# Rearranging the opening of a gated linear attention and SoLU kernel: tables, warm-up, block order, masks and the first load of v

## The chip, the cores and the metric

The kernel runs on one core of a Trainium2 chip. The time is the device time of one execution in microseconds (us). Several executions were timed, and their median is the number to predict. One further execution was recorded by the hardware profiler; its span runs from the first to the last instruction of the core. The engines are named PE (TensorE, matmuls), PEld (its weight loads), DVE (VectorE), ACT (ScalarE), POOL (GpSimd) and SP (SyncE, which issues most DMAs).

## The reference

Two blocks follow each other. The first is a linear attention with a decay for every channel, over 4 batches, 8 heads, 768 tokens and a head dimension of 48. The second is an MLP on the 3072 tokens with 384 inputs and 1024 hidden units.

```python
for t in range(S):
    state = alpha[:, :, t, :, None] * state + np.einsum('bhd,bhe->bhde', k[:, :, t], v[:, :, t])
    y[:, :, t] = np.einsum('bhd,bhde->bhe', q[:, :, t], state)
...
x = np.ascontiguousarray(attn_out.transpose(0, 2, 1, 3)).reshape(B * S, H * D)
h = x @ w_in
e = np.exp(h - h_max)
sm = e / (np.sum(e, axis=-1, keepdims=True) + 1e-09)
solu = h * sm
mu = np.mean(solu, axis=-1, keepdims=True)
var = np.mean((solu - mu) ** 2, axis=-1, keepdims=True)
ln = (solu - mu) / np.sqrt(var + 1e-06) * g_ln
return (ln @ w_out).astype(np.float32)
```

## The kernel before

The 768 tokens are cut into six groups of 128 (`g` is 0 to 5); a group holds all four batches. Inside a group the recurrence is solved in blocks. Alpha is scanned backwards and forwards over the 128 tokens (DVE, line 219). Keys and queries are multiplied by these products. PE forms scores from them (line 278), and a triangular mask is multiplied in (line 289). Then PE reads the values out (line 312), and the state is carried on (line 361). A group's 512 columns then go through the MLP: `up_mm` (line 386), exponential, product and square (lines 400 to 402), and `down` (line 497).

The order of all instructions is written out by hand: each engine runs its own instructions in program order, and semaphores connect the engines. The change lies in the opening, which handles group 0 without anything else to overlap it with.

- SP issues the loads at its start: alpha, k and q in two requests each, of 16 runs of 48 numbers for each of 128 partitions (line 153); then v of the first group in one request of 32 such runs (`load_v_first`, line 188); then six requests for the first half of w_in (`fetch`, line 559), in the form of raw 64-bit numbers. POOL spreads v from its landing place `room` into the tile `vn` by two copies (line 190).
- PE starts with 18 matmuls of ones by ones (`warm(18)`, line 667), of which nothing is read. Each float32 matmul is two MATMUL rows in the trace, each with a LDWEIGHTS.
- `turned` (line 165) transposes a source by matmuls with the identity, 12 blocks of four small matmuls: blocks 0 to 7 are the first 32 channels of the 8 heads, and blocks 8 to 11 the last 16 channels of two heads at once, which ACT first gathers into a tile (`ends_of`, line 158). Three tiles of four blocks each leave: `t[0]`, `t[1]` and `t[2]`. That is done for alpha (`an`), the keys (`kn`) and the queries (`qn`).
- For the queries, DVE takes the three tiles in the order 2, 0, 1 (loop at line 685), with a scan ahead of the last. ACT makes two copies of the ends (`apart`, line 242).
- `scores(0, 0)` and `scores(0, 1)` write four batches of four heads each, into four banks per half. DVE multiplies the mask into all eight tiles (`masked`, lines 698 and 699), and goes on with `bits(0)`, which turns raw 64-bit weights of piece 0 into float32.
- `read_values(0)` reads batch after batch: 16 matmuls each, which need both halves of that batch's `sT`; ACT copies each result to `x` (line 348). Then come `gains` (one small transposition, and `g_col` on DVE), `keys_back` (12 transpositions, three copies by ACT, line 299), `in_range(0)` and `in_range(1)` on ACT (lines 576 and 577), and the loop over eight pieces of the MLP, whose first ACT instruction is the exponential at line 400.

Of the kernel before, what the change touches and what calls it, by code (L numbers as in the profile page):

```python
# [9 lines left out]
FP = mybir.dt.float32  # L10
# [4 lines left out]
ALU = mybir.AluOpType  # L15
AX = mybir.AxisListType
P = 128
# [15 lines left out]
def fast_path(ctx, tc, q, k, v, alpha, moe_w_in, moe_w_out, moe_g_ln, out):  # L33
# [12 lines left out]
    nc = tc.nc  # L46
    B, H, S, D = q.shape
# [4 lines left out]
    NP = H // 2  # L52
    NB = H + NP
# [8 lines left out]
    def pool(name, bufs, **kw):  # L62
        return ctx.enter_context(tc.tile_pool(name=name, bufs=bufs, **kw))
# [5 lines left out]
    small = pool("small", 4)  # L69
# [4 lines left out]
    ps_a = pool("ps_a", 1, space=PS)  # L74
# [4 lines left out]
    mask = const.tile([P, P], FP, name="mask")  # L79
# [7 lines left out]
    mhalf = const.tile([P, 1], FP, name="mhalf")  # L87
# [13 lines left out]
    qn = const.tile([P, H, TQ, D], FP, name="qn")  # L101
# [30 lines left out]
    sT = const.tile([P, B, H, P], FP, name="sT")  # L132
# [13 lines left out]
    def by_token(x):  # L146

        return x.rearrange("p h u d -> p (h u d)").rearrange("p (b h d) -> p b h d", b=B, h=H)
# [9 lines left out]
    def ends_of(src, tag=None):  # L158

        ends = ring.tile([P, T4], FP, name=tag) if tag else two.tile([P, T4], FP, tag="two", name="ends")  # L160
        ends = ends.rearrange("p (b d) -> p b d", b=B)
        nc.scalar.copy(out=ends.rearrange("p b (h d) -> p b h d", h=H), in_=by_token(src)[:, :, :, E0:D])
        return ends

    def turned(src, ends, out, blocks=range(NB)):

        x = by_token(src)
        for j in blocks:
            for b in range(B):
                cols = x[:, b, j, 0:E0] if j < H else ends[:, b, E0 * (j - H) : E0 * (j - H) + E0]  # L170
                nc.tensor.matmul(
                    out[j // NP][32 * b : 32 * b + 32, j % NP], lhsT=cols, rhs=ident, start=True, stop=True,
                    tile_position=(0, 32 * b), skip_group_check=True,
                )
# [9 lines left out]
    def load_v_first(slot):  # L184
        x = slots[slot].rearrange("p (n d) -> p n d", d=D)
        y = vn.rearrange("p b h d -> p (b h) d")
        xi, yi = (z.rearrange("p (n i) d -> p i n d", i=2) for z in (x, y))
        nc.sync.dma_start(out=x, in_=v[:, :, 0:P].rearrange("b h p d -> p (b h) d"))
        for i in range(2):
            nc.gpsimd.tensor_copy(out=yi[:, i, :, all_of[i]], in_=xi[:, i])  # L190

# [92 lines left out]
    masks = {}  # L284

    def masked(half, batches=range(B)):
        a = masks[half]
        for b in batches:
            nc.vector.tensor_tensor(  # L289
                out=sT[:, b, half * NP : half * NP + NP], in0=a[b], in1=mask[:, None, :].to_broadcast([P, NP, P]),  # L290
                op=ALU.mult,
            )
# [25 lines left out]
    def read_begin():  # L318
        reading["y"] = {}
        reading["begun"] = set()  # L320
# [118 lines left out]
    def warm(n, ps=ps_o, tag="o"):  # L439
        t = ps.tile([P, 512], FP, tag=tag, name="warm")  # L440
        for i in range(n):
            nc.tensor.matmul(t[:, 0:P], lhsT=ones, rhs=ones, start=True, stop=True)  # L442
# [209 lines left out]
    nc.gpsimd.memset(seed, 0.0)  # L652
    nc.gpsimd.memset(state, 0.0)
    load_v_first(0)
    fetch(0, 3, 2)
    fetch(2, 1, 2)
# [6 lines left out]
    def three(name, where):  # L663
        return [pool.tile([P, NP, P], FP, tag=tag, name=f"{name}{i}") for i, (pool, tag) in enumerate(where)]


    warm(18)
    t = three("tp_a", [(ps_a, "a0"), (ps_a, "a1"), (ps_a, "a2")])
    turned(an, ends_of(an), t)
    for i in range(3):  # L670
# [2 lines left out]
    t = three("tp_k", [(ps_a, "a3"), (ps_h, "h"), (ps_h, "h")])  # L673
# [5 lines left out]
        nc.vector.tensor_tensor(out=kT[:, part], in0=t[i], in1=hk[:, part], op=ALU.mult)  # L679
    scan_on(0, 0)  # L680
    t = three("tp_q", [(ps_o, "o"), (ps_o, "o"), (ps_a, "a0")])
    turned(qn, ends_of(qn), t)

    warm(2, ps_a, "a1")
    for i in (2, 0, 1):
        if i == 1:
            scan_on(0, i)
# [2 lines left out]
            out=qe if i == 2 else qv[:, part], in0=t[i], in1=aT[:, part, 1:SW], op=ALU.mult  # L690
# [4 lines left out]
    t = [x.tile([P, NP, P], FP, tag=n, name="a_" + n) for x, n in ((ps_h, "h"), (ps_o, "o")) for _ in range(2)]  # L695
    scores(0, 1, t)
    read_begin()
    masked(0)
    masked(1)
    bits(0)  # L700
    read_values(0)
# [6 lines left out]
    for f in range(FC):  # L708
        p = 2 + f // 2
# [215 lines left out]
    def compare(out, x, bound, op):  # L925
# [6 lines left out]
        out=chunks[:, :, 2], in0=sums[:, :, 2], scalar=0.25, in1=sums[:, :, 3], op0=ALU.mult, op1=ALU.is_le  # L932
# [6 lines left out]
    else:  # L939
# [9 lines left out]
        out=bad, in0=all_ok[0:1, 0:1], scalar1=float(P * ends[-1]), scalar2=None, op0=ALU.is_lt  # L949
# [415 lines left out]
def kernel(tc, *args):  # L1365

    with ExitStack() as ctx:
        taken = fast_path(ctx, tc, *args)
    with tc.If(taken > 0):
        general_path(tc, *args)  # L1370
# [30 lines left out]
```

## Time and profile before

| what | value |
|---|---|
| median of 4 executions | 385.36 us (383.77, 383.97, 386.75, 387.59) |
| profiled execution, own time | 386.66 us |
| its span | 384.9 us |
| mean granted TensorE clock | 0.991 of full |
| busy: PE, DVE, ACT, POOL | 370.1, 245.4, 144.3, 125.0 us |
| end of the values' matmuls of group 0 (line 312) | 31.9 us after the start |

The profiled execution is 1.3 us slower than the median, and outside of its span lie 1.76 us. The granted clock is the share of full speed that TensorE's clock was given; it is 1.00 or 0.50 in this trace. A waiting time put down to "issue" is one that no semaphore in the trace explains. A line of the chain gives start, length, engine, tile, line and number of instructions; a line of windows gives for each engine the busy time and, in brackets, the number of instructions, then the granted clock, the DMA share and GB/s.

### The profile page before, as it was taken

What the parts mean: (1) busy time and instruction counts of PE and PEld (TensorE: products, weight loads), DVE (VectorE), ACT (ScalarE), POOL (GpSimd) and SP (SyncE); (2) the same over time, 40 slices, a digit from 0 to 9 for tenths busy, and PEclk for the clock granted to TensorE, in tenths of its full rate; (3) what the DMA queues carried; (4) which work ended last, traced back from release to release, by engine and by line L of the source; (5) the groups of instructions that cost most, each with busy time, mean ns of one, the idle gap of its engine ahead of it and who ended that gap; (6) DMA issues with size and microseconds to landing.
All of it is one profiled execution on the core that took longest, in us unless ns stands there. A gap on an engine that the chain in (4) does not pass through costs nothing.

```text
span 384.9 us, 10525 instructions
## 1 busy us (share of the span) xinstructions
PE 370.1 (96%) x4665; PEld 224.2 (58%) x4665; DVE 245.4 (64%) x381; ACT 144.3 (38%) x258; POOL 125.0 (32%) x132
## 2 busy tenths in 40 slices
PE   8879999879999999999999999999999999999995
PEld 8767335546755656556566555566556665555552
DVE  0986888995989766893665893565885411444410
ACT  2617675284325425224253224252224131333111
POOL 5010000023043991445522544521552620333210
PEclk9999999998999999999999999999999999999999
DMA  9970989402466300963000961000600000000011
GB/s 185 201 289 9 252 242 223 98 0 73 103 139 103 83 4 3 149 148 75 22 3 24 171 148 50 22 4 26 100 0 22 22 24 2 20 21 20 22 43 49
DMA packets 65510, 30.78 MB, mean 80 GB/s; under 512 B 47016, under 2 KB 63664, under 8 KB 65456
## 3 DMA queue, kind: packets, MB, share of 16 engines
q1 hardware_dynamic: 64432, 29.10, 34.4%
q10 hardware_dynamic: 1024, 0.92, 0.7%
q8 instruction: 38, 0.62, 0.7%
q14 instruction: 16, 0.13, 0.1%
HBM read 25.30 MB, written 4.72 MB: 78 GB/s over the span
## 4 chain that ended last, share of the span: by engine, by line
PE 74%; DVE 16%; ACT 3%; issue 2%; DMA 2%; SPq 1%; POOL 0%; DVEq 0%
PE o L497 29%; PE h L386 25%; PE y L312 9%; PE a L278 5%; DVE hT L219 3%; DVE aT L219 3%; DMA an<-in_alpha_dram 2%; PE warm L442 2%; PE kv L361 1%; DVE room L401 1%; DVE sT L289 1%; DVE aT L194 1%; PE tp L297 1%; SPq L141 1%; DVE low L600 1%
## 5 line engine op out<-in xcount | busy, mean ns | idle before, releaser
L497 PE MATMUL o<-w_out,room 128*128 128x385 f32 x384 | 135.4, 496 | 2.4 <-DVE o_mean L523 2.4
L386 PE MATMUL h<-x,w_in 128*128 128x512 f32 x288 | 132.1, 598 | 0.5 <-DVE room L401 0.5
L497 PEld LDWEIGHTS o<-w_out,room 128*128 128x128 f32 x384 | 72.1, 192 | 59.4 <-issue 17.9
L386 PEld LDWEIGHTS h<-x,w_in 128*128 128x128 f32 x288 | 53.0, 190 | 58.9 <-issue 48.1
L401 DVE TENSOR_TENSOR room<-h,e 128x512 f32<-128x512 f32 x40 | 27.6, 690 | 82.2 <-ACT e L400 82.1
L400 ACT ACTIVATE e<-h 128x512 f32<-128x512 f32 x40 | 23.9, 597 | 108.2 <-PE h L386 108.2
L527 POOL TENSOR_TENSOR r<-sums,mhalf 128x1 f32<-128x1 f32 x20 | 14.3, 714 | 141.1 <-DVE sums L519 141.1
L417 POOL TENSOR_TENSOR p<-p,e 128x512 f32<-128x512 f32 x30 | 41.8, 1392 | 15.7 <-ACT e L400 15.7
L402 ACT ACTIVATE u<-room 128x512 f32<-128x512 f32 x40 | 25.2, 630 | 35.2 <-DVE room L401 35.2
L289 DVE TENSOR_TENSOR sT<-a,mask 128x512 f32<-128x512 f32 x44 | 27.3, 683 | 10.5 <-PE a L278 10.4
L219 DVE TENSOR_TENSOR_SCAN hT<-aT,unit 128x516 f32<-128x516 f32 x18 | 23.1, 1347 | 8.7 <-ACT aT L671 8.7
L240 POOL TENSOR_TENSOR kT<-kT,hT 128x1024 f32<-128x1024 f32 (+1 forms) x8 | 14.2, 1793 | 42.4 <-DVE kT L194 34.1
L312 PE MATMUL y<-sT,vn 128*32 128x128 f32 x768 | 25.4, 286 | 2.6 <-issue 1.8
L219 DVE TENSOR_TENSOR_SCAN aT<-aT,seed 128x516 f32<-128x516 f32 x18 | 27.2, 1540 | 0.2
L417 DVE TENSOR_TENSOR p<-p,u 128x512 f32<-128x512 f32 x30 | 23.0, 768 | 6.5 <-ACT u L402 6.5
L278 PEld LDWEIGHTS a<-qv,kT 32*128 32x128 f32 x704 | 22.0, 186 | 8.6 <-issue 2.9
L278 PE MATMUL a<-qv,kT 32*128 32x128 f32 x704 | 25.0, 279 | 1.6 <-DVE qv L689 0.8
L312 PEld LDWEIGHTS y<-sT,vn 128*32 128x32 f32 x768 | 22.6, 115 | 4.9 <-issue 3.6
L211 ACT ACTIVATE sq<-an,mone 128x1536 uint8<-128x1536 f32 x12 | 18.8, 1570 | 0.2
L312 PE MATMUL y<-qv,state 32*32 32x128 f32 x960 | 16.5, 277 | 0.0
L529 ACT ACTIVATE o_sb<-o,r 128x384 f32<-128x384 f32 x16 | 9.3, 580 | 18.7 <-POOL r L527 18.7
L312 PEld LDWEIGHTS y<-qv,state 32*32 32x32 f32 x960 | 12.1, 103 | 6.9 <-issue 4.9
(140 smaller groups left out, 367.5 us busy)
## 6 DMA issues: line engine op xcount, KB each, us to landing
an<-in_alpha_dram SPq DMA_DIRECT2D x20, 192.0 KB, 4.1
vn<-in_v_dram SPq DMA_DIRECT2D x10, 384.0 KB, 5.2
out_dram<-o_sb SPq DMA_DIRECT2D x20, 192.0 KB, 1.9
room<-in_moe_w_in_dram SPq DMA_DIRECT2D x6, 512.0 KB, 8.4
room<-in_moe_w_out_dram SPq DMA_DIRECT2D x8, 384.0 KB, 4.1
kn<-in_k_dram SPq DMA_DIRECT2D x16, 192.0 KB, 4.5
qn<-in_q_dram SPq DMA_DIRECT2D x16, 192.0 KB, 3.9
kn<-in_k_dram SPq DMA_DIRECT2D x4, 384.0 KB, 5.7
```

Of the source, the lines that this page charges most:

```text
L211: nc.scalar.activation(out=sq, in_=x, func=AF.Relu, scale=sign, bias=mone, accum_out=over[:, g, i : i + 1])
L219: nc.vector.tensor_tensor_scan(out=o, data0=a, data1=s, initial=1.0, op0=ALU.mult, op1=ALU.add)
L278: nc.tensor.matmul(a[b][:, i], lhsT=kT[quarter(b), kb], rhs=qv[quarter(b), qb], start=kb == h, stop=kb != h, tile_position=(32 * b, 0), sk ...
L289: nc.vector.tensor_tensor(out=sT[:, b, half * NP : half * NP + NP], in0=a[b], in1=mask[:, None, :].to_broadcast([P, NP, P]), op=ALU.mult,)
L312: nc.tensor.matmul(y_bank(b)[quarter(r), a], lhsT=lhsT, rhs=rhs, start=(b, r) not in begun, stop=stop, tile_position=(row, 32 * r), skip_g ...
L386: nc.tensor.matmul(h, lhsT=w_in[:, a, f * P : (f + 1) * P], rhs=d["x"][:, a].rearrange("p b t -> p (b t)"), start=(a == 0), stop=(a == KC ...
L400: nc.scalar.activation(out=e, in_=h, func=AF.Exp)
L401: nc.vector.tensor_tensor(out=u, in0=h, in1=e, op=ALU.mult)
L402: nc.scalar.activation(out=u2, in_=u, func=AF.Square)
L417: eng.tensor_tensor(out=p, in0=d[0][i] if f == 1 else p, in1=d[f][i], op=ALU.add)
L497: nc.tensor.matmul(d["o"][:, 0 : DM + 1], lhsT=u_of(g, f)[:, b * P : b * P + P], rhs=w_out[:, f], start=(f == 0), stop=(f == FC - 1), skip ...
L527: nc.gpsimd.tensor_tensor(out=r, in0=s[:, 3:4], in1=mhalf, op=ALU.pow)
```

## The change

Four edits, all in the opening.

- ACT copies one column (`mhalf`) to a scratch tile ahead of everything else, so the table load that precedes ACT's first instruction stands before this copy rather than before the gathering of alpha's ends. The warm-up has 16 matmuls, not 18.
- The queries' blocks are turned in the order 0 to 3, 8 to 11, 4 to 7; the warm-up behind them has one matmul, not two.
- Of the eight mask products two, batches 2 and 3 of the first half, leave DVE: ACT copies the scores from PSUM into `sT`, and POOL multiplies the mask in there. DVE does the other six.
- v of the first group is loaded by two requests of two batches each. Their place in SP's order is the same, between q and w_in.

```diff
-        nc.sync.dma_start(out=x, in_=v[:, :, 0:P].rearrange("b h p d -> p (b h) d"))
+        for b in range(0, B, 2):
+            nc.sync.dma_start(
+                out=x[:, H * b : H * b + 2 * H], in_=v[b : b + 2, :, 0:P].rearrange("b h p d -> p (b h) d")
+            )
...
-    warm(18)
+
+    nc.scalar.copy(out=small.tile([P, 1], FP, name="t"), in_=mhalf)
+    warm(16)
...
-    turned(qn, ends_of(qn), t)
-
-    warm(2, ps_a, "a1")
+    turned(qn, ends_of(qn), t, [*range(NP), *range(H, NB), *range(NP, H)])
+
+    warm(1, ps_a, "a1")
...
-    masked(0)
+    for b in (2, 3):
+        s = sT[:, b, 0:NP]
+        nc.scalar.copy(out=s, in_=masks[0][b])
+        nc.gpsimd.tensor_tensor(out=s, in0=s, in1=mask[:, None, :].to_broadcast([P, NP, P]), op=ALU.mult)
+    masked(0, range(2))
     masked(1)
```

## The prediction

> **What bounds the opening now.** I read the page's chain by line first, then the same chain in order of time over the first 60 us, since every edit lies there. Its lines up to the values' end:
>
> ```profile
> 1.05 6.92 PE warm L442 x36
> 7.97 1.05 PE tp_a L171 x32
> ...
> 9.74 3.49 DVE hT L219 x3
> ...
> 19.19 0.94 PE a L278 x22
> 20.14 0.33 issue
> 20.46 1.45 PE a L278 x40
> 21.91 2.11 DVE sT L289 x4
> ...
> 25.03 0.85 PE y L312 x17
> 25.88 1.05 issue
> 26.93 4.92 PE y L312 x105
> ```
>
> PE's warm-up, then DVE's scans and products, then the scores, the masks and the values. At first sight DVE is the engine to relieve: from 9.7 to 20.9 us it has next to no gap, and four masks stand in the chain. But the values do not begin in earnest when a mask is ready. After 21 of their 128 rows PE stops for 1.05 us with no semaphore to wait for ("issue"), and by 26.77, when DVE's last mask ends, everything that they need is there.
>
> What is that stop? I counted MATMUL rows in the timeline. The three unexplained stops of the opening (until 14.03, 20.46 and 26.93) stand behind rows 223 (36 warm, 96 of alpha, 91 of the keys), 350 and 477: 127 apart, which with a LDWEIGHTS to each row makes 254 instructions. The DMA view has a queue of its own for instructions, and the single packets in the trace, 16 KB each, start at 11.45, 17.82 and 24.49 and take 0.9 to 1.4 us: one ahead of each stop by 2.4 to 2.6 us. [...] The next fetch starts 3.8 and 4.0 us after a stop ended while the DMA queues are full (windows of 2 us from 14 to 24: DMA share 0.9 to 1.4), and only 1.1 us after the third, when they have run empty. So from 14 to 27 us a chain of fetches, each started by the block before it, paces PE.
>
> A second thing follows the stop:
>
> ```profile
> 23.70:27.11 3.41, 1.52 (x31) 0.90 (x32) 3.41 (x7) 0.00 (x0) 0.00 (x0) 1.00 0.87 342
> 27.11:30.52 3.41, 3.41 (x72) 3.34 (x67) 3.27 (x5) 0.96 (x2) 0.00 (x0) 0.50 0.04 13
> 30.52:33.93 3.41, 3.41 (x58) 2.94 (x51) 2.55 (x4) 2.27 (x5) 0.00 (x0) 1.00 0.02 5
> ```
>
> These windows are cut where the granted clock changes. PE was busy for 1.52 of 3.41 us (0.45), and the next 3.41 us were granted half the clock: values' rows start every 53 ns there (64 rows) and every 34 ns behind it. The same happened once more, at 85.14, after a window with PE busy for 1.00 us. Windows of 0.71 and 0.73 busy (16.87 and 13.46) were not followed by it.
>
> The last view is what takes the values over:
>
> ```profile
> DVE g_col L613 <- PE tp_g L612: 0.8, 1, 0.8
> DVE room L401 <- ACT sT L400: 2.0, 1, 2.0
> 34.06 0.95 ACT L576 ACTIVATE sq<-room 128x768 f32<-128x768 f32 x1
> 36.10 0.97 ACT L576 ACTIVATE sq<-room 128x768 f32<-128x768 f32 x1
> 38.03 0.58 ACT L400 ACTIVATE sT<-h 128x512 f32<-128x512 f32 x1
> ```
>
> Behind the values DVE waits 0.8 us for `g_col` and 2.0 us for the first exponential, whereas ACT runs from the x copy at 31.88 to 38.03 with one gap of 0.26. So what counts for the rest is when PE ends the values (31.85), not when DVE ends its masks; DVE has 2.8 us to spare. From there on all shifts together: SP's next request (37.18) waits for ACT's line 576, the alpha load behind it is in the chain from 47.69, and the initial loads end at 27.9.
>
> **Part by part.**
>
> *Warm-up and table load.* Alpha lands at 6.57. ACT then loads its table, 1.28 us, before `ends` at 7.87. Now the load runs before 5 us, behind ACT's four DMA issues (which end at 2.8), beside the DMA: `ends` is done at 7.2, not 8.5. Of that nothing is on the path: PE needs `ends` only for its third tile at 9.57, and ACT stood idle for 0.56 us before its copy at 9.05, waiting for PE. What gives is the shorter warm-up: rows start every 213 ns until 6.6 and every 111 ns behind it (13 start in 6.5 to 7.9), so four rows less are 4 x 0.111 = 0.45 us. The warm-up then ends near 7.5, still behind alpha's landing, so PE has no gap there and the clock opens as before. DVE's run begins at 9.3.
>
> *Order of the queries.* `qe` needs the tile of blocks 8 to 11, which PE ends at 17.7, just when DVE's scan ends (17.74). With DVE 0.45 earlier this would be late by 0.4; in the new order the tile is there at about 16.8 (q lands at 14.89 in either kernel; 64 rows from there take 1.9 us). So this edit keeps the 0.45, and adds nothing. PE's first wait for `qv` ends at 18.6, not 19.04, if nothing else is late. One warm matmul less lies in this wait (18.35 to 19.19): nothing.
>
> *Fetches.* Three matmuls less are 6 rows less, so the boundaries fall 6 rows later: in row 28 of the scores and row 27 of the values. The block that starts the chain of fetches is entered at what was row 96 and is now row 100 of the old count, with PE 0.45 ahead: 4 rows at 30 ns (tp_a: 32 in 1.05 us is 33) eat 0.13, so the chain moves by 0.3. The third block comes at about 26.6 instead of 26.93, and 6 rows fewer are left behind it: 6 x 0.034 = 0.2. Sum: the values end 0.5 us earlier.
>
> *Masks.* DVE loses two rows of 0.60 each (four masks take 2.49), 1.2 us. ACT gains two copies of 0.58 (line 671, same shape) in a stretch where it is idle (19.8 to 27.9). POOL gains two products: 1.26 to 1.88 us each by line 417, which has the same shape, beside a busy DVE. They queue behind the v copies, which end at 21.95 or earlier. Scores of batches 2 and 3 are ready near 21.6, so `sT` is ready at 25.4, at worst 26.4; its first reader would come at about 27.6. No stall. The only instruction queued behind POOL's products is a 0.12 us memset for a later group. DVE's masks end at 25.6 to 25.9; the values wait for the block until 26.6, so the masks bring nothing unless the fetch comes sooner.
>
> *v in two requests.* v's single issue took 3.23 us, the next one (w_in) 3.38; a request of half the size took 1.75 (q). In the window 13 to 14 the DMA share fell to 0.24: v's packets begin at about 14.0, when its whole issue is through. Two requests begin near 12.5 and fill this dip, so v and w_in land up to 1.3 us sooner, v at about 19 instead of 20.36. SP's issues become two of 1.75 in place of one of 3.23, 0.3 us more, and w_in's first request then sits behind one half as long (1.75, not 3.38), so the six end no later. Its reader, PE's first value at 23.78, is 1.8 us behind the POOL copy already: nothing gained. It could shorten the third fetch if the queues emptied before 24.5; they would at 26.6, so no.
>
> Where the trace is silent, the fetch under the new load, I bound it by its own rows: a start 1.1 us after the stop before (empty queues, a gain of 2.9 more) and one later by the spread of the two loaded ones (0.2 us, a loss). I take the loaded value, because the share of 1.0 stays up to 26 us.
>
> **Sum.** On the profiled execution: 386.66 - 0.5 = 386.2. It lies 1.3 above the median and holds two half-clock windows; of the four times two are near 383.9 and two near 387.2, as if such windows come in some executions. On the median: 385.36 - 0.5 = **384.9 us**.
>
> [...]
>
> **The rivals.**
>
> *The masks count (0.30).* If the third fetch comes earlier than reckoned, the values start when masks are ready, and PE's gap shrinks. For it: DVE's masks are in the chain, and v's earlier end leaves less traffic. Against it: three equal intervals. Gain 1.5 to 3.5 us with the half clock gone in more executions: 383.0 likeliest, and in the upper end past 1%.
>
> *The clock closes more often (0.15), slower.* The place is the window around 24 to 27. Scores end and masks begin earlier, but the block still comes at 26.6, so PE's idle time stays near 1.9 of 3.41 us or grows by 0.1. [...] Sliding a 3.41 us window over the trace gives shares of 0.45 to 0.71 here, by where it falls. If the deciding share is near 0.55, a little more idle time makes the half clock come in most executions and not in some. Price: 64 rows x (53 - 34) ns = 1.2 us, up to 1.7 (half of the window); less 0.5 that is gained: 386.3. It decides from where PE's busy share in the window drops below about one half in more executions than before.
>
> *Nothing arrives (in the likeliest case's range).* If the 0.3 of the fetch does not come, 0.2 remain: 385.2.
>
> **How the numbers follow.** The case of the paced fetch has 0.55; its own range is 383.7 to 386.0, the executions' spread included. Two half-clock windows come or not with each execution, so a median moves by 1.5 us on its own. The range is 382.2 to 386.9: it takes in most of the first rival and the slower one. One per cent, 3.9 us, is about what a measurement of this kernel can tell from no change. Faster by more than that needs the upper end of the first rival, 3.5 us, and executions without the other half-clock window (386.66 - 3.5 - 1.7 = 381.5): 0.15. Slower by more: the clock and a late POOL product together: 0.08. Within: 0.77.
>
> **What would show it.** Right: unexplained stops of PE near row 28 of the scores and row 27 of the values, ending near 20.1 and 26.6, masks done a good half us before the latter, and DVE still waiting for the first exponential, longer than 2.0 us. ACT's table load before 5 us, alpha's scans from 9.3, v landed near 19. Wrong: values running through from 24 us on (the masks count), or POOL as releaser of a value's matmul, or half a clock where before there was none.

## The result, and the profile after

The changed kernel is faster: the ratio of its times to those of the kernel before is 0.9957, with a 95% interval of 0.9944 to 0.9969. The medians are 383.07 us (42 executions, 382.36 to 384.61) and 384.29 us (63 executions, 383.48 to 389.65). Forecast were 384.9 us and a gain of 0.5 us; measured was a gain of 1.2 us by the medians and 1.7 us by the ratio. The direction and the range were right, the size was too small. The 383.07 lies outside of the likeliest case's own range (383.7 to 386.0) and close to the number of the first rival (383.0), whose mechanism, the masks, the runs below do not bear out; that agreement is luck. The forecast also stood on a median of four executions, two of them near 387 us; with 63 it came out 1.1 us lower.

The profiled execution of the changed kernel took 382.35 us, with a span of 380.6 us. It holds no half-clock window ahead of its last instruction (mean granted clock 1.000), where that of the kernel before held two (0.991). So the two profiles differ by 4.3 us, far more than the kernels do, and have to be read with care.

The timeline of the changed kernel, PE, then ACT and DVE (start, length, engine, line, operation; in brackets the idle time before it and what ended it):

```profile
18.00 2.07 PE L281 MATMUL a<-qv,kT 32*128 32x128 f32 x64 [0.19 <-DVE qv L694]
...
21.84 0.41 PE L315 MATMUL y<-sT,vn 128*32 128x128 f32 x4
22.68 1.07 PE L315 MATMUL y<-sT,vn 128*32 128x128 f32 x23 [0.42 <-DVE sT L292]
24.71 3.04 PE L315 MATMUL y<-sT,vn 128*32 128x128 f32 x101 [0.97 <-issue]
...
2.81 1.28 ACT L671 ACT_TABLE_LOAD   x1 [2.81 <-issue]
...
7.87 0.58 ACT L676 COPY aT<-tp_a 128x512 f32<-128x512 f32 x1 [0.51 <-PE tp_a L171]
...
16.57 0.69 DVE L694 TENSOR_TENSOR qe<-tp_q,aT 128x512 f32<-128x512 f32 x1
...
24.68 0.95 DVE L592 TENSOR_SCALAR top<-room 128x768 uint32<-128x768 uint32 x1 [0.26 <-DMA room<-in_moe_w_in_dram]
...
33.94 0.58 ACT L403 ACTIVATE sT<-h 128x512 f32<-128x512 f32 x1
```

The stop in the values stands where it was reckoned, behind 27 of the 128 rows (4 and 23), and all that the remaining 101 rows read is there before it ends (POOL's second product ends at 23.34, DVE's last mask at 24.42, the stop at 24.71). No semaphore explains it; a single 16 KB packet of the instruction queue starts 2.5 us ahead of its end, at 22.21, and takes 1.08 us. The stop ends earlier than the 26.6 that was forecast, and DVE's masks are done 0.3 us ahead of that, not a good half. The stop in the scores, at row 22 before, is gone: the 64 rows of the first half run through. The scores start at 18.00, not 19.19, and the values end near 27.7, not 31.85. ACT runs from there to the first exponential, as before: from the start of the values' last row (27.48) to the exponential (33.94) it is 6.46 us, in the kernel before 6.46 as well (31.57 and 38.03). DVE waits for w_in for 0.26 us, which it did not before. Its wait for the first exponential was to be longer than the 2.0 of before; it is 0.82 us.

The same kernel in the windows around the values:

```profile
22.15:25.56 3.41, 2.02 (x57) 1.64 (x58) 3.15 (x5) 0.38 (x1) 1.26 (x2) 1.00 0.96 322
25.56:28.97 3.41, 3.41 (x91) 3.19 (x81) 3.27 (x5) 1.98 (x5) 0.00 (x0) 1.00 0.41 166
```

PE was busy for 2.02 of 3.41 us (0.59), and the clock stayed full; in the kernel before, a share of 0.45 (1.52 of 3.41 us, to 27.11) was followed by half a clock.

### The profile page after: what moved, and what is told of

It is laid out like the page before. It is cut to its first block, busy times and chain, and to the rows that moved or that the text cites. A ratio compares the mean times of both kernels' runs of the same rounds, so it can differ in the third digit from the quotient of the medians.

```text
span 380.6 us, 10523 instructions
## 1 busy us (share of the span) xinstructions
PE 366.3 (96%) x4659; PEld 220.7 (58%) x4659; DVE 244.4 (64%) x379; ACT 145.9 (38%) x261; POOL 127.5 (33%) x134
## 4 chain that ended last, share of the span: by engine, by line
PE 66%; DVE 17%; SPq 5%; ACT 4%; DMA 3%; issue 3%; POOL 0%; DVEq 0%; ACTq 0%
PE o L500 29%; PE h L389 24%; PE y L315 7%; PE a L281 4%; SPq L153 3%; DVE aT L222 3%; DVE room L404 2%; DMA room<-in_moe_w_in_dram 2%; DVE hT L222 2%; DVE top L595 2%; DVE low L603 1%; DVE top L592 1%; DMA an<-in_alpha_dram 1%; DVE aT L197 1%; PE kv L364 1%
## 5 line engine op out<-in xcount | busy, mean ns | idle before, releaser
L500 PE MATMUL o<-w_out,room 128*128 128x385 f32 x384 | 133.6, 491 | 2.4 <-DVE o_mean L526 2.4
L292 DVE TENSOR_TENSOR sT<-a,mask 128x512 f32<-128x512 f32 x42 | 26.1, 683 | 9.1 <-PE a L281 9.1
L315 PE MATMUL y<-sT,vn 128*32 128x128 f32 x768 | 23.8, 274 | 1.9 <-issue 1.5
L315 PEld LDWEIGHTS y<-sT,vn 128*32 128x32 f32 x768 | 21.1, 110 | 4.1 <-issue 3.3
```

The costliest lines, as they stand in the source:

```text
L292: nc.vector.tensor_tensor(out=sT[:, b, half * NP : half * NP + NP], in0=a[b], in1=mask[:, None, :].to_broadcast([P, NP, P]), op=ALU.mult,)
L315: nc.tensor.matmul(y_bank(b)[quarter(r), a], lhsT=lhsT, rhs=rhs, start=(b, r) not in begun, stop=stop, tile_position=(row, 32 * r), skip_g ...
L500: nc.tensor.matmul(d["o"][:, 0 : DM + 1], lhsT=u_of(g, f)[:, b * P : b * P + P], rhs=w_out[:, f], start=(f == 0), stop=(f == FC - 1), skip ...
```

## The experiments

Twelve kernels, each against the kernel before. In the first eight one edit is undone in the changed kernel ("undo"), or only some are made in the kernel before ("only"). The last four follow up. Besides the ratio I give what the clock tells. Each execution's mean granted clock is on record, and an execution with two or more half-clock windows has, by estimate, about 0.991 or less: half of a window of 3.41 us is 0.0045 of a span of 382, and the profile of the kernel before, with two, has 0.991. (The figure does not say where the half clock lies; the last 0.1 us of the changed kernel's span have a mean of 0.71 as well.) Such executions come in 30% of the runs of the kernel before (60 of 199) and take 386.96 us in the mean, while the other 139 take 384.31 (384.27, 384.33 and 384.33 in the three groups of four kernels beside which they were timed). The changed kernel has none in 44.

| kernel | ratio (95%) | clock 0.991 or less | mean of the others, us |
|---|---|---|---|
| before | 1 | 60 of 199 | 384.31 +- 0.11 |
| changed | 0.9957 (0.9944 to 0.9969) | 0 of 44 | 383.14 +- 0.16 |
| undo masks | 0.9953 (0.9937 to 0.9968) | 0 of 21 | 383.09 +- 0.17 |
| undo v | 0.998 (0.9954 to 1.0005) | 2 of 14 | 383.14 +- 0.38 |
| undo order | 0.9979 (0.9959 to 1.0) | 0 of 14 | 383.79 +- 0.29 |
| undo warm-up and table | 0.9981 (0.9964 to 0.9999) | 2 of 22 | 383.69 +- 0.25 |
| undo table | 0.9958 (0.9941 to 0.9975) | 0 of 22 | 383.46 +- 0.21 |
| only warm-up and table | 0.9983 (0.9968 to 0.9997) | 0 of 22 | 384.22 +- 0.26 |
| only order | 0.9974 (0.995 to 0.9998) | 7 of 22 | 383.60 +- 0.28 |
| only warm-up, table, order | 0.9955 (0.9936 to 0.9974) | 0 of 22 | 383.27 +- 0.30 |
| only masks | 0.9998 (0.9975 to 1.0021) | 6 of 22 | 384.34 +- 0.32 |
| only v | 1.0004 (0.9979 to 1.0029) | 2 of 14 | 384.21 +- 0.29 |
| only warm-up, table, masks | 0.9965 (0.9945 to 0.9984) | 1 of 21 | 383.69 +- 0.25 |
| only warm-up, table, v | 0.9967 (0.995 to 0.9984) | 0 of 22 | 383.92 +- 0.12 |

The last column's +- is 1.96 standard errors, worked out from the single times. "At full clock" below means the executions of this column; five of the eleven such profiles (mean clock 0.993 to 0.996, the others 0.999 or 1.000) still hold one half-clock window, at 81 to 83 us.

### Undo the masks

```diff
-    for b in (2, 3):
-        s = sT[:, b, 0:NP]
-        nc.scalar.copy(out=s, in_=masks[0][b])
-        nc.gpsimd.tensor_tensor(out=s, in0=s, in1=mask[:, None, :].to_broadcast([P, NP, P]), op=ALU.mult)
-    masked(0, range(2))
+    masked(0)
     masked(1)
```

> The changed kernel with all eight mask products on DVE again. Paced-fetch theory (the values start in earnest when PE's third instruction block arrives): DVE's masks end 1.2 us later, near 24.6 to 25.5 us, at or just behind the block's arrival, so the time moves by 0 to 0.3 us against the changed kernel (ratio to the kernel before 0.996). Mask theory (DVE's masks and the weight conversion behind them set the path): 1.0 to 1.2 us are lost, ratio 0.999. Clock theory (the gain is that fewer executions have half-clock windows): PE's idle time before the values grows, and the share of executions with two such windows rises toward that of the kernel before.

Nothing was lost (383.09 against 383.14). The profile shows why, PE and then DVE:

```profile
22.46 0.41 PE L315 MATMUL y<-sT,vn 128*32 128x128 f32 x4
23.84 1.07 PE L315 MATMUL y<-sT,vn 128*32 128x128 f32 x23 [0.98 <-DVE sT L292]
25.66 1.61 PE L315 MATMUL y<-sT,vn 128*32 128x128 f32 x50 [0.74 <-issue]
...
24.30 1.28 DVE L292 TENSOR_TENSOR sT<-a_o,mask 128x512 f32<-128x512 f32 x2
```

The values' first wait for a mask is longer (0.98 against 0.42 us), and the stop put down to "issue" behind it is shorter (0.74 against 0.97). The four rows ahead of the mask and the 23 behind it are used up early enough in both; the next block is what the rest waits for (its packet starts at 22.73 here and at 22.21 in the changed kernel).

### Undo the split of v

```diff
-        for b in range(0, B, 2):
-            nc.sync.dma_start(
-                out=x[:, H * b : H * b + 2 * H], in_=v[b : b + 2, :, 0:P].rearrange("b h p d -> p (b h) d")
-            )
+        nc.sync.dma_start(out=x, in_=v[:, :, 0:P].rearrange("b h p d -> p (b h) d"))
```

> The changed kernel with v in one request again. Paced-fetch theory: v is not read before 22 us, so 0 us, ratio 0.996. Rival: the single request leaves the DMA queues empty near 13 to 14 us, so w_in's first piece lands up to 1.3 us later, and with DVE's masks out of the way the conversion of piece 0 waits for it: 0.5 to 1.3 us lost, ratio 0.997 to 0.999, with a wait of DVE for w_in of 1 us or more in the profile (0.26 us in the changed kernel).

The wait for w_in came as the rival had it, and cost nothing. DVE of this kernel, then ACT:

```profile
25.55 0.96 DVE L589 TENSOR_SCALAR top<-room 128x768 uint32<-128x768 uint32 x1 [0.93 <-DMA room<-in_moe_w_in_dram]
...
34.16 0.58 ACT L400 ACTIVATE sT<-h 128x512 f32<-128x512 f32 x1
```

DVE's conversion starts 0.9 us later than in the changed kernel, yet the exponential follows the values' last row (27.76) by the same 6.4 us. DVE's slack behind the values takes it up: its wait for the exponential falls from 0.82 to 0.17 us. Two of 14 executions had the low clock, which makes the ratio's interval wide; the others take what the changed kernel takes.

### Undo the order of the queries

```diff
-    turned(qn, ends_of(qn), t, [*range(NP), *range(H, NB), *range(NP, H)])
+    turned(qn, ends_of(qn), t)
...
-    warm(1, ps_a, "a1")
+    warm(2, ps_a, "a1")
```

> The changed kernel with the queries' blocks in plain order and two warm matmuls behind them. Paced-fetch theory: DVE waits up to 0.4 us for the tile of the ends, but the third block's time stays, so 0 to 0.2 us. Engine-chain theory: 0.4 to 1.0 us lost, ratio 0.997 to 0.998, since q's tile for the ends comes last and the scores start later by that.

0.65 us were lost (383.79 against 383.14): the engine-chain theory. DVE of this kernel, and then of the kernel before:

```profile
15.44 1.22 DVE L222 TENSOR_TENSOR_SCAN aT<-aT,seed 128x516 f32<-128x516 f32 x1
17.55 0.69 DVE L694 TENSOR_TENSOR qe<-tp_q,aT 128x512 f32<-128x512 f32 x1 [0.89 <-PE tp_q L171]
...
16.52 1.22 DVE L219 TENSOR_TENSOR_SCAN aT<-aT,seed 128x516 f32<-128x516 f32 x1
17.76 0.69 DVE L689 TENSOR_TENSOR qe<-tp_q,aT 128x512 f32<-128x512 f32 x1
```

DVE is through with its scan at 16.7 and waits 0.89 us for the tile of the ends, which in plain order is the last of the three. The scores start at 18.99, 1.0 us later than in the changed kernel, and the values' last row starts at 28.16, 0.7 later.

### Undo the warm-up and the table load

```diff
-    nc.scalar.copy(out=small.tile([P, 1], FP, name="t"), in_=mhalf)
-    warm(16)
+    warm(18)
```

> The changed kernel with 18 warm matmuls and the table load where it was. Paced-fetch theory: 0.5 us lost (0.45 of the warm-up and 6 rows, of which 4 are these), ratio 0.997. Engine-chain theory: the same 0.45, or up to 1.2 us in executions whose clock opens early, because there the warm-up ends before the table load would. Clock theory: more executions with a second half-clock window, ratio 0.998 to 1.000.

0.55 us (383.69 against 383.14), as both theories had it, so this run does not tell them apart. The low clock came in two of 22, too few to be told from none.

### Only the warm-up, the table load and the order

> The kernel before with the two edits whose undoing cost something: 16 warm matmuls with the table load ahead, and the queries' blocks in the new order; masks on DVE and v in one request as before. Theory of the two edits (0.55 and 0.67 us lost when undone, and nothing for masks): the whole shift of the median, 1.2 to 1.4 us, ratio 0.9965 or below. Rival (all four are needed together): 0.5 us or less, ratio 0.9985.

The whole gain, with the masks on DVE and v in one request: 383.27 us, ratio 0.9955. In its profile there is not even a stop in the values:

```profile
21.91 0.41 PE L312 MATMUL y<-sT,vn 128*32 128x128 f32 x4
23.31 3.98 PE L312 MATMUL y<-sT,vn 128*32 128x128 f32 x124 [0.98 <-DVE sT L289]
```

Here the third fetch started at 21.93, 1.4 us ahead of the values' 124 rows, and PE ran through without a stop at row 477; the values wait for the masks alone (0.98 us). So the block and the masks are near each other, and which of them comes last changes with the execution. DVE has no slack left here: it starts the first product at 34.22 without a wait, where the exponential has ended at 33.98.

### Only the masks

> The kernel before with only the two masks moved to ACT and POOL. Paced-fetch theory: 0 us, since the values wait for the block; ratio 0.999 to 1.001. Mask theory: up to 1.2 us gained, ratio 0.997. Clock theory: a shorter gap of PE before the values, so fewer executions with a mean clock of 0.991 or less (about one in four in the kernel before), without a change of the others.

Nothing (ratio 0.9998), and six of 22 executions with the low clock. The profiled one is such a case. Its windows, and then its timeline of PE:

```profile
22.46:25.87 3.41, 1.68 (x41) 1.02 (x34) 2.91 (x6) 0.00 (x0) 2.03 (x3) 1.00 0.94 316
25.87:29.29 3.42, 2.09 (x41) 2.05 (x43) 3.28 (x5) 0.48 (x1) 0.00 (x0) 0.50 0.37 146
29.29:32.70 3.41, 3.41 (x72) 3.34 (x65) 0.59 (x1) 0.96 (x2) 0.00 (x0) 0.50 0.00 0
```

```profile
23.71 0.85 PE L312 MATMUL y<-sT,vn 128*32 128x128 f32 x17 [0.42 <-DVE sT L289]
27.20 5.91 PE L312 MATMUL y<-sT,vn 128*32 128x128 f32 x107 [2.64 <-issue]
```

The masks are early (the values go on at 23.71, not 25.03), and PE then stands for 2.64 us put down to "issue". The third fetch started at 24.80, 2.4 us ahead of its end. The clock halves from 25.87 on, within the stop, for two windows, and the values end later than in the kernel before.

### Only v

> The kernel before with only v in two requests. Paced-fetch theory: 0 us in most executions, ratio 0.999 to 1.001. Rival: without the dip of the DMA queues at 13 to 14 us the second and third instruction fetch start earlier (17.8 and 24.5 us in the kernel before, 13.4 and 22.2 in the changed one), which takes the stop in the scores away: second fetch before 16 us, no unexplained stop at row 350, and fewer executions at 386 us and above.

Nothing (384.21 against 384.31). In its profile there is no stop in the scores and the second fetch is early (14.7), as the rival had it; but there is none either in the other kernels with v in one request, except the kernel before (second fetch at 13.5 to 16.3), so v is not the reason.

### Only the warm-up and the table load

> The kernel before with only the 16 warm matmuls and the table load ahead of them. Paced-fetch theory: 0.3 to 0.5 us gained, ratio 0.9987. Engine-chain theory: nothing or 0.1, since the tile of the ends, last in the plain order, then holds DVE (a wait of about 0.4 us before the queries' first product).

At full clock 0.1 us, within the error (384.22), with DVE waiting 0.96 us for the tile of the ends: this half of the change needs the order.

```profile
17.48 0.69 DVE L690 TENSOR_TENSOR qe<-tp_q,aT 128x512 f32<-128x512 f32 x1 [0.96 <-PE tp_q L171]
```

But none of 22 executions had the low clock, and that is enough for the ratio of 0.9983 (30% of 2.65 us are 0.8 us in the mean).

### Only the order

> The kernel before with only the queries' new order and one warm matmul behind it. Theory now (the start of the scores is handed on one to one; it is the later of DVE's scan and the queries' tile of the ends, so the order alone leaves DVE's side as the limit): scores start 0.1 to 0.5 us earlier, 0.3 to 0.7 us gained in executions of full clock, ratio 0.998; with two half-clock windows in at least one execution in ten. Rival (order and warm-up are worth their time independently, about 0.7 and 0.5): 0.7 us, and the same share of half-clock executions as before, one in four.

0.7 us at full clock, and the low clock as often as before (7 of 22). So the order is worth its time alone, as the rival had it; the rival's other half, 0.5 us for warm-up and table alone, did not come (0.1). The profiled execution had its third fetch at 25.44 and the low clock as well.

### Undo the table load alone

> The changed kernel with the table load back behind alpha's landing, and 16 warm matmuls. If only the warm-up's length counted, 0 us (ratio 0.9957). If the table load holds ACT's copy of the first tile once the warm-up ends early (alpha at 6.6, load and gathering to 8.5, against a first tile at 7.8 to 8.5): 0.1 to 0.7 us lost, by the moment at which the clock opens, ratio 0.9965.

0.3 us at full clock (383.46 against 383.14), at the edge of the errors. The profile shows the place: ACT gathers until 8.65, while the first tile's last matmul has ended by then, and the two copies follow without a gap.

```profile
6.73 1.28 ACT L162 ACT_TABLE_LOAD   x1 [6.73 <-DMA an<-in_alpha_dram]
7.19 1.95 PE L171 MATMUL tp_a<-ident,an 128*32 128x128 f32 x64
8.03 0.62 ACT L162 COPY ends<-an 128x512 f32<-128x512 f32 x1
8.55 1.25 ACT L675 COPY aT<-tp_a 128x512 f32<-128x512 f32 x2
```

In the changed kernel the copy follows PE's start by 1.15 us (6.72 to 7.87), here by 1.36.

### Warm-up and table with the masks, and with v

> The kernel before with the shorter warm-up, the table load ahead and the two masks moved; order and v as before. Undoing the order alone left 0.6 us of gain, doing warm-up and table alone gave 0.1 in executions of full clock: either the masks make the difference (ratio 0.998 here, and 0.5 us in executions of full clock), or v does (then 0.1 us here), or it is chance (0.1 to 0.4 us).

> The kernel before with the shorter warm-up, the table load ahead and v in two requests; order and masks as before. If v makes the difference named for the kernel with the masks: ratio 0.998 and 0.5 us in executions of full clock; otherwise 0.1 us.

These two were to settle why undoing the order left 0.5 us of gain at full clock while warm-up and table alone gave 0.1. With the masks it is 0.6 us (383.69), with v 0.4 (383.92). So both look worth something while the order is the old one, and nothing once the new order is in (undo masks, undo v, and only warm-up, table and order). The errors of 0.1 to 0.3 us don't allow more than that, and no trace showed the mechanism; it stays open.

## Why the prediction was right in direction and small in size

The steps in the order of the prediction. The fetch times are the starts of the single packets of 16 KB in the traces' instruction queue, and "block" stands for what such a packet brings. Each row is one execution.

| profile | scores start | 2nd fetch | 3rd fetch | values resume | values' last row | first exponential |
|---|---|---|---|---|---|---|
| before | 19.19 | 17.82 | 24.49 | 26.93 | 31.57 | 38.03 |
| changed | 18.00 | 13.41 | 22.21 | 24.71 | 27.48 | 33.94 |
| undo masks | 18.62 | 15.44 | 22.73 | 25.66 | 28.42 | 34.87 |
| undo order | 18.99 | 13.60 | 23.07 | 25.39 | 28.16 | 34.65 |
| undo warm-up and table | 19.31 | 15.50 | 23.42 | 25.71 | 28.55 | 35.01 |
| only warm-up, table, order | 18.08 | 13.65 | 21.93 | no stop | 27.01 | 33.40 |
| only v | 19.01 | 14.70 | 22.93 | 25.31 | 28.28 | 34.70 |
| only masks | 19.08 | 15.85 | 24.80 | 27.20 | 32.84 | 39.30 |
| only order | 18.89 | 16.30 | 25.44 | 27.83 | 33.33 | 39.91 |

*What decides is the end of the values, not DVE's masks or the conversion.* Right. The exponential follows the start of the values' last row by 6.4 to 6.6 us in every profile of the table, with DVE late or early. Undoing the masks cost nothing, and making only them gained nothing. But DVE's 2.8 us to spare were read from an execution with late values. With early ones its wait for the exponential is 0.82 us in the changed kernel and none with warm-up, table and order alone, so what else is saved ahead of the values will meet DVE.

*The boundaries are fixed in the count of PE's instructions and move by 6 rows.* Right: the stop is behind row 27 of the values in the changed kernel, and behind row 21 to 25 in those with more warm matmuls, at PE's row 477 wherever it came.

*"So from 14 to 27 us a chain of fetches, each started by the block before it, paces PE."* This step failed. It was read from one execution, in which the stops ended 6.4 and 6.5 us apart (14.03, 20.46, 26.93), and that was one of the late ones. In all thirteen other profiles the second fetch starts between 13.4 and 16.3 us, ahead of the scores (18.0 or later in the table), and there is no stop at row 350. In the eleven with the full clock in the values the third fetch follows the start of the scores by 3.6 to 4.5 us, and in nine of these PE then stops and goes on 2.2 to 2.9 us after the packet's start. So the values did wait for the third block, but its fetch kept its distance to the scores and not to the fetch before it (6.7 to 9.5 us in the table), and what makes the scores earlier is handed on, within that spread of 0.9 us. What starts a fetch, no run shows. The shift of the third block, 0.3 in the sum, should have been that of the scores' start.

*"So this edit keeps the 0.45, and adds nothing."* This is the term that was missed. I let DVE's scan and the tile of the ends be even (17.74 and 17.7), so that only the warm-up could shift the pair. But the tile goes with the landing of q (14.69 in "undo order" with 16 warm matmuls, 14.89 in the kernel before with 18) and not with the warm-up: in plain order PE ends it at 17.43 to 17.71 us in all seven profiles, with 16 warm matmuls or 18. DVE's scan ends at 16.5 to 17.7 there, earlier with the shorter warm-up (16.5 in "only warm-up and table" and 16.7 in "undo order", 17.7 in the kernel before), and the tile is last in all but the kernel before, where both are even. The warm-up's own pace moves too: its rows go from one every 213 ns to one every 111 at 6.6 us in the profile of the kernel before and at 5.1 in that of the changed kernel. In the new order the tile is done at 16.5 to 17.2, ahead of the scan in all seven. So the even pair was that of one execution in which the pace changed late. Measured at full clock, the order is worth 0.7 us alone and 0.65 undone. Shorter warm-up and earlier table are worth 0.1 alone and 0.55 when undone in the changed kernel. Together 1.0 to 1.2: the order gains alone, the warm-up and table only once the tile is out of the way.

*"Of that nothing is on the path", of the table load.* Mostly right in the profile of before, where the warm-up's pace changes at 6.6: alpha's matmuls start at 7.90 and the gathering ends at 8.49. In "undo table" they start at 7.19, and the gathering behind the late table load ends at 8.65. 0.3 us measured.

*The warm-up gives 0.45.* The changed kernel's alpha matmuls start at 6.72 in its profile, and at 8.14 in "undo warm-up and table" with 18 warm matmuls; but in that pair the change of pace moved too, from 5.1 to about 7.1 (an estimate: 15 warm rows take the 2.54 us from 5.67, at 213 and then 111 ns each). The 0.55 of undoing both parts fits the 0.45, yet less the 0.3 of the table it leaves 0.2, with an error of 0.3; no run has the longer warm-up with the early table.

*Masks on POOL and v in two requests at nothing.* Right. POOL's two products took 2.50 us, the lower of the two estimates (twice 1.26), and no PE matmul waited for them as its last releaser. v's spreading began at 19.07, as forecast.

*The rivals.* "The masks count" did not come, though its premise did: the third fetch was earlier than reckoned. But PE still stopped behind row 477 (0.97 us), and undoing the masks cost nothing. The 3.5 us at the upper end of its gain no run shows: the most at full clock was 1.2 us, with the masks on POOL (383.14) or on DVE (383.09). "The clock closes more often" came the other way round, and this is the second part of the gain: the low clock went from 30% of the executions to none of 44, which at 2.65 us each is, by estimate, 0.8 us in the mean beside the 1.2 at full clock (1.7 by the ratio for both). Across all kernels here it came in 77 of 279 executions with 18 warm matmuls (before, undo warm-up and table, and only order, only masks, only v), and in 3 of 202 with 16 (the changed kernel and all others; 0 of 22 with the late table load among them, against 2 of 22 with 18 and the same other edits, too few to settle it by that pair). In the three profiles that had a half clock in the values (before, only masks, only order) the third fetch is late, at 24.5 to 25.4 us, and in all the others it is at 23.4 or earlier. So the late third block and the half clock go together. Why the block is late in some executions is open: the order alone started the scores earlier (18.89 against 19.19) and kept the share (7 of 22). The fourteen profiles give a lead. The three late third fetches are those with the latest second ones (15.85, 16.30 and 17.82 us, 15.50 at most in the others), and the second is early (13.4 to 13.7) in the six in which the first starts at 9.2 to 9.4. All six have 16 warm matmuls; in the five with 18 the first starts at 10.5 to 11.5. No run moved a fetch by itself, so this is not shown to be the cause.

The second half-clock window, at 85 us, I had put at 1.7 us in the bounds. It costs little: from the first exponential to the end it was 346.8 us in the kernel before with that window, 346.7 in the changed kernel without, and 346.8 to 347.9 in the other profiles of the table, with and without.

That a busy share near 0.55 of the window ahead decides the half clock, the condition of the slower rival, is not shown. For it: in "only masks" the window up to 25.87 holds 1.3 us of the stop, with PE busy for 1.68 of 3.41 us (0.49), in "only order" the one up to 26.73 has 0.85 us (0.25), and half the clock followed both. Against it: in the changed kernel a window with 1.64 us (0.48) was followed by the full clock, and in "only masks" one with 2.09 us (0.61), at half the clock already, by another half. The windows of the changed kernel:

```profile
76.76:80.17 3.41, 1.64 (x20) 1.29 (x12) 3.19 (x8) 3.01 (x8) 0.00 (x0) 1.00 0.00 0
80.17:83.59 3.42, 2.80 (x9) 1.48 (x9) 3.39 (x4) 3.20 (x7) 3.29 (x4) 1.00 0.15 58
```

## What to carry to other kernels

Where an operand becomes ready by the later of two chains, cutting the earlier one shows nothing until the later one is cut as well: find both arrival times in the trace, and which of them the edit moves. Count the instructions of an engine against the profile's instruction packets before unexplained stops are put down to data (here the stops of the kernel before lie 127 rows apart, and a 16 KB packet starts 2.4 to 2.6 us ahead of the end of each). And look at the granted clock of every execution before you build a sum on one profile: here a stop and its half clock, which came in three of ten executions, looked like the kernel's structure.

## What the runs showed that was not expected

- PE went on with a block 2.2 to 2.9 us after its instruction packet started, wherever it stopped for the third one, and in three profiles the packet itself started late (5.3 to 6.6 us after the scores' start against 3.6 to 4.5). In "only masks" a third fetch at 24.8 us came with a stop of 2.64 us in the middle of the values' matmuls, which the trace puts down to no semaphore.
- How often the clock halves changed with the warm-up at the very start, 20 us ahead of the place: 77 of 279 executions with 18 warm matmuls, 3 of 202 with 16. (The kernels differ in other edits too.)
- The stop of 2.64 us in "only masks" cost more than itself: the values' 107 rows behind it took 5.91 us, at a granted clock of 0.50 up to 32.70, where 101 rows of the changed kernel took 3.04 at 1.00.
